# The feed-forward's weight loads moved to GpSimd's queue, and one string of TensorE's order replaced

## The chip, the cores and the metric

The kernel runs on one core of a Trainium2 chip. The metric is device time in microseconds (us), the median of several runs. A core has five engines with instruction streams of their own: TensorE (PE; its weight loads are shown as PEld), VectorE (DVE), ScalarE (ACT), GpSimd (POOL) and SyncE (SP). They wait for one another by semaphores. Transfers between the chip's main memory and the core are issued by an instruction on one of these engines; in this kernel mostly by SyncE, a few by ScalarE and GpSimd. An engine works through its own instructions strictly in order, so a transfer whose wait is not over holds what stands behind it on that engine.

## The reference

Two rounds of a recurrent attention layer and a gated feed-forward layer, with the same weights in both rounds:

```
x = x + A(layernorm(x));  x = x + B(layernorm(x))
x = x + A(layernorm(x));  x = x + B(layernorm(x))        x: 1 x 2048 x 576, bf16

A: 64 segments of 32 tokens, one after the other; mem is 8 x 576
   h = concat(mem, segment)                 40 tokens
   q, k, v = h Wq, h Wk, h Wv               32 heads of 128
   p = softmax(mask(q k^T / sqrt(128)));  o = (p v) Wo
   mem = o[:8];  output = o[8:]

B: out = (silu(x w1) * (x w3)) w2           576 -> 4608 -> 576
```

The memory of 8 tokens makes the 64 segments of one attention layer a chain. The two rounds can overlap: the second round can work on a segment once the first round has finished it.

## The kernel before

**Steps.** Both rounds run interleaved. At step t the first round works on segment t and the second on segment t - 8, so there are 72 steps; in 56 of them both rounds are present. A step goes through the 32 heads in four groups of eight. For each group TensorE makes q and k (`QK`), the scores (`SC`), the product of the softmax with v (`PV`) and the output projection (`WO`). Between `SC` and `PV` the softmax runs: VectorE adds the mask and subtracts the maximum, ScalarE takes the exponential, VectorE sums and writes the normalised result into the tile PB, and PB is transposed into the tile PTS. In steps with both rounds that transpose is a DMA transpose issued by SyncE (`ptr_dma`, line 1223). After it has landed, GpSimd clears PB again (`pb_zero`, line 1213). PB and PTS have two buffers each.

**Feed-forward.** Every four steps a job (`job`) puts 128 tokens of each round through the feed-forward. The 4608 hidden columns are cut into 18 pairs of 256 columns. For each pair three nodes load weights: `W13` (two transfers of 512 rows of 256 columns, from w1 and w3), `W13t` (two transfers of the last 64 rows) and `W2l` (one transfer of 256 rows of 576 columns). So a job has 90 weight transfers. The tiles `w13`, `w13t` and `w2` have two buffers each, so the load of a pair waits until TensorE is through with the pair two before it. In the trace the tiles of w1 and w3 stand as W<-in_B_w_dram, that of w2 as W2C<-in_B_w_dram. The last job is different: its weights go into the room of the attention weights (`tail_load`).

**Order.** A planner (`plan`) fixes the order of all instructions before the program is built. Every piece of work is a node with an engine, a duration, a latency `lat` after its end and a priority. TensorE's order is not planned but written out as a string, one letter for each node: Q and q for the q and k products, S for scores, P for `PV`, O and o for `WO`, F and f for a pair's products with w1 and w3, W and w for the products with w2, G, g, V and v for the products that make v, n, a and b for the transposes after a layer norm, p for the attention output's transposes. The whole string is FIRST, then eleven times FOUR, then LAST. FOUR is one period: four steps and one job, 208 letters. The other engines' nodes are put, one after the other, where they can start soonest by the planner's durations; among those that can start, the one with the lowest priority number goes first. `TRLAT` is the latency that the planner gives a DMA transpose after its 1.25 us on the queue. The chip keeps the order of every engine; the times are then its own.

**Queues.** SyncE issues the weights at the start, the feed-forward's weights, the DMA transposes and most loads of x. GpSimd computes the power in the layer norms (`ln_pow`, line 889), clears PB, loads the residual XR and stores finished output (line 719). TensorE's instructions stand under line 704, ScalarE's under 707, VectorE's under 710, SyncE's transfers under 713: these lines are helpers that every operation goes through, so the tiles tell operations apart.

Of the kernel before, what the change touches and what calls it, by code (L numbers as in the profile page):

```python
# [13 lines left out]
P = 128  # L14
R64 = 64
D = 576
# [16 lines left out]
R_HT = 6  # L33
PTR = 112
PRE = ()
TRLAT = 3.0
AHEAD = True
BACK = 4
GATES = {1: "WO1", **{i: "WO3" for i in range(2, 8)}}
# [177 lines left out]
def ewh(*ns):  # L217
# [11 lines left out]
    "SQQqqqQSbQGSgqqQPQGSgOPGggOPGwOoPooOo"  # L229
)  # L230
FOUR = (
    "QQppQqqqqQvVSnSnQFfqqQQFqqffFQWSwPSFffPFOOWowoPFffPOOwoFoWQQQqqqfFSFqqfqQQQwSWGSFqfqgQQPGSfggwGPFPOGWogOPOOoooFV"
    "vfqqQQWQQqqfSFSqqQQwQSFffqqFQPwOSWPFFPoffOOwPWOoooFqqfqQQWQQSaqqQSbqqqQQQSwSGggGPGPOoggGPOPOOooo"
)
LAST = (
    "QqqqppQQQqSvVSnnQQqqfFSqqQPQFSffOPFOwPWFOfFoPoofOoWQQQqqqwSQFQqqfGSqgQQPQqfSFGgqgPGSWwfFOFPOfgGOwoPOoooqqqQQQQqS"
# [9 lines left out]
class Opt:  # L246

    qk, qkt, sc, tr, pv, wo, wog, vm = 0.0079, -0.0342, 0.0268, 0.1447, 0.0406, 0.2653, 0.0725, 0.1407
    vmt, vx, vxt, ff, fft, win, w2, gstep = -0.0231, 0.2313, 0.0843, 0.2124, -0.1839, 0.8 * (LAG - 4), 0.1943, 0.0624
# [3 lines left out]
def make_nodes(em, nseg, pools, o=Opt, dma_bw=230e3, load_bw=380e3, tail_bw=330e3):  # L253
# [4 lines left out]
    def node(*a, **k):  # L258
        n = Node(*a, **k)
        n.prio += 1e-9 * len(nodes)  # L260
        nodes.append(n)
        return n
# [27 lines left out]
    b = banks(1)  # L290
# [208 lines left out]
    def job(j):  # L499
# [24 lines left out]
        def units(pps, at0, end):  # L524
            for at, pp in enumerate(pps, at0):
                mids, w2s, htts, lds = [], [], [], []
                stays = last and pp == npp - 1
                in_tail = end and not stays
                for pr_ in (2 * pp, 2 * pp + 1):
                    prio = (s0 + 4 if end and not last else s0) + o.ff + (o.win if s0 + 4 < nst else o.last_win) * (2 * at + pr_ % 2) / NPR  # L530
                    if stays:
                        w13, w13t, w2 = kept[pr_]
                        ld = ldt = []
                        w2s.append(w2)
                    elif in_tail:
                        w13 = w13t = w2 = None
                        ld = ldt = tail[pp]
                    else:
                        keep = before_last and pp == npp - 1
                        w13, w13t, w2 = Slot("w13", users=1 + keep), Slot("w13t", users=1 + keep), Slot("w2", users=ne + keep)  # L540
                        kept[pr_] = w13, w13t, w2
                        after = stored if j == 0 else first_ld[:1]
                        ld = [node("DMA", 0.98, em.load_w13(pr_, w13), deps=after, prio=prio - 1, acq=[w13], lat=3.1, name="W13")]
                        ldt = [node("DMA", 1.03, em.load_w13t(pr_, w13t), deps=after, prio=prio - 0.995, acq=[w13t], lat=3.0, name="W13t")]
                        first_ld.extend(ld)
                        lds.append(node("DMA", 0.45, em.load_w2(pr_, w2), deps=after, prio=prio - 0.99, acq=[w2], lat=2.95, name="W2l"))
                        w2s.append(w2)
                    b = banks()
                    htt = Slot("htt", users=ne)
# [130 lines left out]
class Emitter:  # L680
# [34 lines left out]
    def adma(self, out, in_):  # L715
        self.ch("ACT", self.nc.scalar.dma_start(out=out, in_=in_))

    def swdma(self, out, in_):
        self.ch("POOL", self.nc.gpsimd.dma_start(out=out, in_=in_))

# [85 lines left out]
    def load_w13(self, pr, w13):  # L806
        def f(n):
            fa = pr * 2 * P
            W = self.T.W13[:, w13.i]
            for kind, wd in ((0, self.a.w1), (1, self.a.w3)):  # L810
                self.dma(W[:, 4 * kind:4 * kind + 4], wd[0:4 * P, fa:fa + 2 * P].rearrange("(c p) f -> p c f", p=P))
        return f

    def load_w13t(self, pr, w13):
        def f(n):
            fa = pr * 2 * P
            for kind, wd in ((0, self.a.w1), (1, self.a.w3)):
                self.dma(self.T.W13[kind * R64:(kind + 1) * R64, w13.i, 8], wd[4 * P:D, fa:fa + 2 * P])
        return f

    def load_w2(self, pr, w2):
        fa = pr * 2 * P
        return lambda n: self.dma(self.T.W2C[:, w2.i], self.a.w2[fa:fa + 2 * P, :].rearrange("(b p) d -> p b d", p=P))

    def tail_load(self, i, what, gate):

# [739 lines left out]
```

## Time and profile before

| | |
|---|---|
| median of 3 runs | 2702.18 us (2692.01 to 2706.06) |
| profiled execution | 2702.11 us, its span 2700.2 us |
| mean granted TensorE clock | 0.987 |
| TensorE busy | 2582.1 us, 96% |
| VectorE busy | 2039.5 us, 76% |
| ScalarE busy | 1202.9 us, 45% |
| GpSimd busy | 334.3 us, 12% |
| transfers | 371.40 MB, 138 GB/s |

All rows below come from one profiled execution. A row of a timeline gives the start in us from the span's beginning, the length in us, the engine (a q behind it means that its sequencer issues a transfer), the line, the operation, the tiles as written<-read, the shape, and how many instructions were merged; a square bracket tells how long the engine stood idle before it and what ended that. A row of waits gives the engine that waited, what it waited for, the us in total, how often, and the longest. A row of a tile gives an engine, its operation and tiles, how many, and the least, median and greatest length in ns. A row of transfers gives tiles, the issuing engine, how many, KB each, and the median us from issue to landing. A row of stretches gives start and end, the length, the busy time of PE, PEld, DVE, ACT and POOL (with their instructions), the granted TensorE clock in parts of one, the share of the DMA engines that was busy, and GB/s. The chain that ended last is followed back from the last instruction; its shares are of the whole span.

### The profile page before, as it was taken

Reading aid. Unit: us, or ns where it says so; the run is one execution under the profiler, and the core shown is the slowest. Engines: PE = TensorE matmul, PEld = TensorE weight load, DVE = VectorE, ACT = ScalarE, POOL = GpSimd, SP = SyncE. Lnnn points to the kernel's source line nnn. Section 1 sums busy time; section 2 is a strip of 40 time slices with the busy share of each in tenths; the row PEclk is TensorE's granted clock in tenths of the full one; section 3 lists DMA queues with packets and bytes.
Section 4 is the critical chain, followed back from the end, with each engine's and each line's share of the span. In section 5 each row is a group of like instructions: output and inputs, shape, how many; then the busy total and the mean of one; then the engine's idle time right before and its main releaser. Section 6 shows DMA issues by size and latency. Waiting matters only on the chain.

```text
span 2700.2 us, 132038 instructions
## 1 busy us (share of the span) xinstructions
PE 2582.1 (96%) x58710; PEld 2202.3 (82%) x58766; DVE 2039.5 (76%) x5185; ACT 1202.9 (45%) x3447; POOL 334.3 (12%) x399
## 2 busy tenths in 40 slices
PE   6999999999999999999999999999999999999998
PEld 4787878888788888888888888887888888888876
DVE  4777777777777777787777877777777787787876
ACT  2554443434444343454535444453444445344443
POOL 1111011101101111110111101011110101011110
PEclk8999999999999999999999999999999999999999
DMA  9056745666544654555475655546555654554458
GB/s 312 8 163 157 170 88 139 137 144 137 115 128 103 163 131 127 149 114 129 111 165 125 148 129 124 135 106 153 124 146 130 130 134 102 128 146 124 130 149 247
DMA packets 690428, 371.40 MB, mean 138 GB/s; under 512 B 234328, under 2 KB 682592, under 8 KB 689216
## 3 DMA queue, kind: packets, MB, share of 16 engines
q1 hardware_dynamic: 686320, 355.08, 53.4%
q8 instruction: 459, 7.52, 1.2%
q0 software_dynamic: 3024, 6.93, 0.9%
q10 hardware_dynamic: 512, 0.94, 0.2%
q14 instruction: 113, 0.93, 0.1%
HBM read 306.72 MB, written 2.36 MB: 114 GB/s over the span
## 4 chain that ended last, share of the span: by engine, by line
PE 74%; DMA 9%; DVE 9%; issue 2%; SPq 1%; ACT 1%; POOL 0%; DVEq 0%; POOLq 0%; ACTq 0%
PE bank L704 74%; DMA PTS<-PB 7%; DVE HTT L710 2%; DVE PB L710 1%; DVE STAT L710 1%; DMA XN<-in_A_x_dram 1%; DVE SME L710 1%; DVE V L710 1%; SPq L713 1%; DVE XR L710 1%; DVE LNS L710 0%; DMA W<-in_B_w_dram 0%; DVE OT L710 0%; DVE QKT L710 0%; DMA W2C<-in_B_w_dram 0%
## 5 line engine op out<-in xcount | busy, mean ns | idle before, releaser
L704 PEld LDWEIGHTS <-W 128*128 128x128 bf16 (+2 forms) x32272 | 1253.0, 100 | 127.8 <-issue 67.9
L704 PE MATMUL bank<-HT,W 128*128 128x80 bf16 (+3 forms) x23040 | 784.8, 197 | 19.6 <-ACT HT L707 7.3
L704 PE MATMUL bank<-XTB,W 128*64 128x256 bf16 (+5 forms) x9232 | 667.6, 264 | 4.6 <-DMA W<-in_B_w_dram 2.7
L1213 POOL MEMSET PB<- 128x1024 bf16 x288 | 273.1, 952 | 1846.0 <-DMA PTS<-PB 1033.3
L707 ACT ACTIVATE QKT<-bank 128x192 bf16<-128x192 f32 (+2 forms) x1473 | 348.2, 323 | 303.8 <-PE bank L704 301.4
L704 PE MATMUL bank<-OT,WO 128*128 128x80 bf16 (+3 forms) x11520 | 418.7, 199 | 4.1 <-ACT OT L707 2.8
L704 PEld LDWEIGHTS <-WO 128*128 128x128 bf16 (+1 forms) x11520 | 389.0, 103 | 31.3 <-issue 20.8
L707 ACT ACTIVATE V<-bank 64x512 bf16<-64x512 f32 (+1 forms) x575 | 326.8, 586 | 188.7 <-PE bank L704 180.8
L704 PE MATMUL bank<-WV,HT 128*32 128x512 bf16 (+5 forms) x3442 | 363.5, 385 | 10.2 <-DMA WV<-in_A_Wv_dram 4.6
L707 ACT ACTIVATE HTT<-bank 128x512 bf16<-128x512 f32 (+1 forms) x324 | 176.3, 549 | 338.4 <-PE bank L704 333.3
L704 PE MATMUL bank<-W2C,HTT 128*64 128x288 bf16 (+1 forms) x2992 | 323.6, 287 | 1.7 <-DVE HTT L710 0.4
L707 ACT ACTIVATE OT<-bank 128x320 bf16<-128x320 f32 (+2 forms) x406 | 156.5, 399 | 296.8 <-PE bank L704 292.5
L710 DVE TENSOR_TENSOR PB<-SME,STAT 40x128 bf16<-40x128 f32 (+4 forms) x912 | 274.9, 336 | 15.5 <-POOL PB L1213 5.9
L710 DVE TENSOR_REDUCE STAT<-SME 104x8 f32<-104x320 f32 (+1 forms) x576 | 273.3, 474 | 14.9 <-ACT SME L707 7.7
L710 DVE SCALAR_TENSOR_TENSOR XR<-bank,XR 128x288 f32<-128x288 f32 x574 | 245.6, 448 | 50.4 <-PE bank L704 46.3
L704 PEld LDWEIGHTS <-HT 128*32 128x32 bf16 (+4 forms) x3496 | 151.5, 98 | 147.2 <-issue 39.9
L704 PEld LDWEIGHTS <-HTT 128*64 128x64 bf16 (+1 forms) x3072 | 225.6, 104 | 47.2 <-issue 7.6
L710 DVE SCALAR_TENSOR_TENSOR HTT<-HTT,bank 128x512 bf16<-128x512 bf16 (+1 forms) x324 | 201.4, 622 | 72.6 <-ACT HTT L707 69.3
L710 DVE CAST V<-bank 64x512 bf16<-64x512 f32 (+1 forms) x289 | 197.8, 685 | 61.2 <-PE bank L704 55.6
L710 DVE TENSOR_TENSOR HTT<-HTT,bank 128x512 bf16<-128x512 bf16 (+1 forms) x324 | 203.4, 628 | 28.1 <-PE bank L704 0.5
L707 ACT ACTIVATE SME<-SME 104x320 f32<-104x320 f32 (+1 forms) x288 | 135.2, 469 | 144.3 <-DVE SME L710 140.8
L710 DVE CAST QKT<-bank 128x128 bf16<-128x128 f32 (+4 forms) x447 | 124.8, 327 | 82.0 <-PE bank L704 80.9
(59 smaller groups left out, 1409.6 us busy)
## 6 DMA issues: line engine op xcount, KB each, us to landing
W<-in_B_w_dram SPq DMA_DIRECT2D x608, 256.0 KB, 3.7
W2C<-in_B_w_dram SPq DMA_DIRECT2D x304, 288.0 KB, 3.5
W<-in_B_w_dram SPq DMA_DIRECT2D x608, 32.0 KB, 3.2
W<-in_B_w_dram SPq DMA_DIRECT2D x16, 512.0 KB, 8.5
WO<-in_A_Wo_dram SPq DMA_DIRECT2D x4, 1152.0 KB, 10.3
XR<-in_A_x_dram POOLq DMA_DIRECT2D x16, 288.0 KB, 3.2
WV<-in_B_w_dram SPq DMA_DIRECT2D x8, 576.0 KB, 7.2
W<-in_A_Wq_dram SPq DMA_DIRECT2D x16, 256.0 KB, 6.7
```

Of the source, the lines that this page charges most:

```text
L704: self.ch("PE", self.nc.tensor.matmul(out, lhsT=lhsT, rhs=rhs, start=start, stop=stop, skip_group_check=True, **k))
L707: self.ch("ACT", self.nc.scalar.activation(*a, **k))
L710: self.ch("DVE", getattr(self.nc.vector, fn_)(*a, **k))
L713: self.ch("SP", self.nc.sync.dma_start(out=out, in_=in_))
L1213: return lambda n: self.ch("POOL", self.nc.gpsimd.memset(self.T.PB[:, pb.i, 0:GROUPS[g][1]], 0.0))
```

## The change

Three constants, the string FOUR, and one new function. The 90 weight transfers of a job, and those of all jobs but the last one's own loads, are issued by GpSimd (`swdma`) and no longer by SyncE (`dma`). Their nodes stand in the planner under POOL with durations 1.2, 1.2 and 0.6 us (`LT`) for `W13`, `W13t` and `W2l`. `TRLAT` goes from 3.0 to 2.2. FOUR is another string of the same letters in the same numbers; FIRST and LAST stay. The buffers, the computation and the last job's loads stay. Every other engine's order follows from the planner, so it moves too.

```
-TRLAT = 3.0
+TRLAT = 2.2
+LOADS = "POOL"
+LT = (1.2, 1.2, 0.6)
...
 FOUR = (
-    "QQppQqqqqQvVSnSnQFfqqQQFqqffFQWSwPSFffPFOOWowoPFffPOOwoFoWQQQqqqfFSFqqfqQQQwSWGSFqfqgQQPGSfggwGPFPOGWogOPOOoooFV"
-    "vfqqQQWQQqqfSFSqqQQwQSFffqqFQPwOSWPFFPoffOOwPWOoooFqqfqQQWQQSaqqQSbqqqQQQSwSGggGPGPOoggGPOPOOooo"
+    "QQppQqqqqQVvSnnSQFqqffFQQQSqqWwPFPOOffoFSFoPwWffFOFPwOWooFqffQQQQqqqWSwSqqQQQQfqgqGSFPFfgGOSPFogfgGGPOOPWwOoooFv"
+    "VfqqQQQwWQfqqSFSQQQfqqqFSFqfPQwOSWoPFffOFPwOPWOoooFfqqqQQWQQSaqqQSbqqqQQQSGSgggGPGPOwGogPOPOOooo"
 )
...
-                        ld = [node("DMA", 0.98, em.load_w13(pr_, w13), deps=after, prio=prio - 1, acq=[w13], lat=3.1, name="W13")]
-                        ldt = [node("DMA", 1.03, em.load_w13t(pr_, w13t), deps=after, prio=prio - 0.995, acq=[w13t], lat=3.0, name="W13t")]
+                        ld = [node(LOADS, LT[0], em.load_w13(pr_, w13), deps=after, prio=prio - 1, acq=[w13], lat=3.1, name="W13")]
+                        ldt = [node(LOADS, LT[1], em.load_w13t(pr_, w13t), deps=after, prio=prio - 0.995, acq=[w13t], lat=3.0, name="W13t")]
...
-                        lds.append(node("DMA", 0.45, em.load_w2(pr_, w2), deps=after, prio=prio - 0.99, acq=[w2], lat=2.95, name="W2l"))
+                        lds.append(node(LOADS, LT[2], em.load_w2(pr_, w2), deps=after, prio=prio - 0.99, acq=[w2], lat=2.95, name="W2l"))
...
+    def wdma(self, out, in_):
+        (self.swdma if LOADS == "POOL" else self.dma)(out, in_)
...
-                self.dma(W[:, 4 * kind:4 * kind + 4], wd[0:4 * P, fa:fa + 2 * P].rearrange("(c p) f -> p c f", p=P))
+                self.wdma(W[:, 4 * kind:4 * kind + 4], wd[0:4 * P, fa:fa + 2 * P].rearrange("(c p) f -> p c f", p=P))
```

`load_w13t` and `load_w2` change from `self.dma` to `self.wdma` in the same way.

More of the change, by code (lines that the diff above doesn't have):

```diff
@@ L817, in f @@
             for kind, wd in ((0, self.a.w1), (1, self.a.w3)):
-                self.dma(self.T.W13[kind * R64:(kind + 1) * R64, w13.i, 8], wd[4 * P:D, fa:fa + 2 * P])
+                self.wdma(self.T.W13[kind * R64:(kind + 1) * R64, w13.i, 8], wd[4 * P:D, fa:fa + 2 * P])
         return f
@@ L822, in load_w2 @@
         fa = pr * 2 * P
-        return lambda n: self.dma(self.T.W2C[:, w2.i], self.a.w2[fa:fa + 2 * P, :].rearrange("(b p) d -> p b d", p=P))
+        return lambda n: self.wdma(self.T.W2C[:, w2.i], self.a.w2[fa:fa + 2 * P, :].rearrange("(b p) d -> p b d", p=P))
     def tail_load(self, i, what, gate):
```

## The prediction

> **What bounds the kernel now.** I read the page first (busy times, then the chain that ended last), then the stretches of the steady part, then TensorE's waits there.
>
> ```profile
> PE 2582.1 (96%) x58710; PEld 2202.3 (82%) x58766; DVE 2039.5 (76%) x5185; ACT 1202.9 (45%) x3447; POOL 334.3 (12%) x399
> PE bank L704 74%; DMA PTS<-PB 7%; DVE HTT L710 2%; DVE PB L710 1%; DVE STAT L710 1%; DMA XN<-in_A_x_dram 1%; DVE SME L710 1%; DVE V L710 1%; SPq L713 1%; DVE XR L710 1%; DVE LNS L710 0%; DMA W<-in_B_w_dram 0%; DVE OT L710 0%; DVE QKT L710 0%; DMA W2C<-in_B_w_dram 0%
> ```
> ```profile
> core 0: us, PE busy (x) PEld busy (x) DVE busy (x) ACT busy (x) POOL busy (x), PEclk, DMA share, GB/s
> 618.50:2188.80 1570.30, 1530.26 (x33020) 1311.45 (x33060) 1201.09 (x3031) 703.98 (x2120) 187.45 (x220) 0.99 0.56 132
> 778.70:939.70 161.00, 155.22 (x3302) 132.57 (x3306) 120.29 (x304) 70.40 (x212) 18.68 (x23) 0.98 0.55 129
> 1251.30:1405.60 154.30, 151.92 (x3303) 130.53 (x3307) 120.10 (x304) 70.27 (x212) 18.55 (x22) 1.00 0.58 133
> ```
> ```profile
> PE bank L704 <- DMA PTS<-PB: 28.7, 17, 3.8
> PE bank L704 <- ACT HT L707: 3.4, 10, 0.3
> ```
>
> TensorE bounds it: 96% busy, 74% of the chain. The largest transfer in the chain is the transpose of the softmax result (PTS<-PB, 7%). The first stretch is ten of the eleven repeats of the period: 157.0 us each, 153.0 busy, 4.0 idle. The last fence is TensorE's waits in that stretch: 28.7 of the 40.0 idle us are waits for that transpose, the next wait is 3.4. The other two stretches are a slow and a quick period. The slow one is busy 155.2 us against 151.9 for the same instructions, at a granted clock of 0.98 against 1.00; so what idles TensorE also seems to cost clock. All ten lie (1530.3 - 1519.2) / 10 = 1.1 us above the quick one in busy time.
>
> Why the transpose is late shows in SyncE's queue, with VectorE and TensorE beside it, in one period:
>
> ```profile
> 1656.74 1.22 SPq L1223 DMA_TRANSPOSE PTS<-PB  x1
> 1658.08 5.09 SPq L713 DMA_DIRECT2D W<-in_B_w_dram  x8
> 1663.28 1.26 SPq L1223 DMA_TRANSPOSE PTS<-PB  x1
> ```
> ```profile
> 1657.46 1.13 DVE L710 TENSOR_TENSOR PB<-SME,STAT 40x128 bf16<-40x128 f32 x4
> ```
> ```profile
> 1655.31 1.91 PE L704 MATMUL bank<-XTB,W 128*128 128x256 bf16 x16
> 1657.15 0.46 PE L704 MATMUL bank<-HT,W 64*128 64x80 bf16 x16
> 1660.88 1.15 PE L704 MATMUL bank<-W2C,HTT 128*128 128x288 bf16 x8
> 1668.60 0.71 PE L704 MATMUL bank<-PTS,V 128*128 128x80 bf16 x8 [2.39 <-DMA PTS<-PB]
> ```
>
> PB is written by 1658.59, but SyncE is issuing eight weight loads (5.09 us) and comes to the transpose at 1663.28, 4.7 us late. TensorE then stands for 2.39 us. In the period before it is the same place, with 1.77 us:
>
> ```profile
> 1502.13 4.77 SPq L713 DMA_DIRECT2D W<-in_B_w_dram  x8
> 1512.04 0.46 PE L704 MATMUL bank<-PTS,V 128*128 128x80 bf16 x8 [1.77 <-DMA PTS<-PB]
> ```
>
> **The change, part by part.** The sum is made against the profiled execution: 2702.1 us with a span of 2700.2; the median of the runs is 2702.2, so no correction.
>
> *1. SyncE's queue loses 1520 loads.* The stall above goes: I take 2.0 us a period, between 1.77 and 2.39. It is 20 of the 28.7 us in ten periods. What is late next is the rest, 0.9 us a period, from transposes that were issued in time and landed late. Of the 1.1 us of busy time lost with the clock I give back the same share, 0.8. Gain 2.8 us a period; bounds 0 (something else ends the wait at the same moment) and 2.9 + 1.1 = 4.0.
>
> *2. The order.* The letters of the period are the same 208, so TensorE's work is the same. Counting array shapes along the two orders, 63 changes of shape become 61. One costs about 0.1 us: sixteen matmuls of 256 columns, at an estimated 0.11 us, fill 1.73 of the 1.84 us between 1655.31 and 1657.15. So 0.2 us. The new order was made with a latency after a transpose of 2.2 us instead of 3.0, so products with V stand about 1 us nearer behind their scores. That eats slack and is priced under 3.
>
> *3. GpSimd gets the loads.* Their price there is not in the trace; the nearest rows are its own transfers, and SyncE's of several shapes:
>
> ```profile
> L719 POOL DMA_DIRECT2D out_dram<-XN x15: 549/552/594, 538.8 to 2667.3; - x15
> L713 SPq DMA_DIRECT2D out_dram<-XN x2: 366/372/377, 2697.1 to 2697.6; - x2
> L713 SPq DMA_DIRECT2D W<-in_B_w_dram x1248: 367/514/2909, 48.1 to 2685.1; - x179
> L713 SPq DMA_DIRECT2D W2C<-in_B_w_dram x304: 367/421/1792, 54.5 to 2648.9; - x152
> L1213 POOL MEMSET PB<- x288: 946/952/961, 32.3 to 2652.4; 128x1024 bf16 x144
> XR<-in_A_x_dram POOLq DMA_DIRECT2D x16, 288.0 KB, 3.2
> PTS<-PB SPq DMA_TRANSPOSE x224, 3.9
> ```
>
> GpSimd's own have 128 runs and take 0.55 us. The w1 and w3 loads have 512 runs, their tails 64, w2 256. If a load costs the same whatever its runs, it is 0.55 us; if all of it goes with the runs, 2.2, 0.28 and 1.1. On SyncE the least of both groups of weight loads (367 ns) is that of the 128-run store (366), so I take a value near flat: 0.6 to 0.8 us. A period has 18 x 5 = 90 loads: 54 to 72 us, on top of GpSimd's 18.7, in 154. At the other end it is 36 x 2.2 + 36 x 0.28 + 18 x 1.1 = 109 us. Neither fills the engine, so the price lies in who stands behind the loads.
>
> The Trainium skill, "DMA: Bandwidth & Descriptors", section "Anatomy of one DMA", says that many descriptors can be emitted before their incremental cost shows; its "SBUF — State Buffer", section "SBUF: two separate sides", warns that VectorE in a two-port mode keeps GpSimd from writing descriptors. By the first the sum stands at the forecast below; by the second it goes to rival B. The trace agrees with the first so far: beside a VectorE that is busy 76%, GpSimd's stores stay within 549 to 594 ns and its memsets within 946 to 961.
>
> Behind the loads stand the memsets that clear PB (16 a period), the power of the layer norms, the loads of XR and the stores. PB has two buffers, so in a burst of four groups the next softmax waits for the memset:
>
> ```profile
> 1591.40 1.85 POOL L1213 MEMSET PB<- 128x1024 bf16 x2 [29.81 <-DVE STAT L710]
> 1592.38 0.11 DVE PB L710
> ```
>
> The chain that ended last runs from the first memset (1591.40 + 0.96) straight into VectorE's next write of PB. In GpSimd's order in the changed program, memsets stand right behind four to twelve loads, 2 to 7 us of issue at 0.6. The same kind of hold on SyncE (4.7 us) reached TensorE with 2.39, half. A memset is one step further away, so I take 0.8 us a period for memset delays and for the nearer products together; bounds 0 and 2.4 (one such place in each period as bad as the old one).
>
> Steady part: -2.8 - 0.2 + 0.8 = -2.2 us a period, x 11 = -24.
>
> *4. The parts whose order is not searched anew.* From 149 to 618 us TensorE waits 12.5 us for transposes, after 2188.8 it waits 1.8:
>
> ```profile
> PE bank L704 <- DMA PTS<-PB: 12.5, 10, 3.9
> PE bank L704 <- DMA PTS<-PB: 1.8, 2, 1.3
> ```
>
> With the 70% of part 1, 9 to 10 us could go; the loads fall where that order did not foresee them on GpSimd, so I take 4. Bounds -12 and +8 (0.8 us more in ten such stretches).
>
> *5. The start.* Nothing holds the first ten loads on GpSimd any more, whereas SyncE had them behind all attention weights:
>
> ```profile
> 39.94 8.10 SPq L713 DMA_DIRECT2D WO<-in_A_Wo_dram  x4
> 48.08 6.40 SPq L713 DMA_DIRECT2D W<-in_B_w_dram  x4
> 5.47 0.30 POOL L1519 MEMSET maskb<- 8x40 bf16 x2
> 11.52 0.56 POOL L889 TENSOR_TENSOR LNS<-LNS,mhalf 128x1 f32<-128x1 f32 x1 [5.75 <-DVE LNS L710]
> 36.74 1.04 PE L704 MATMUL bank<-WV,HT 128*32 128x512 bf16 x8 [1.84 <-DMA WV<-in_A_Wv_dram]
> W<-in_B_w_dram SPq DMA_DIRECT2D x608, 256.0 KB, 3.7
> GB/s 312 8 163 157 170 88 139 137 144 137 115 128 103 163 131 127 149 114 129 111 165 125 148 129 124 135 106 153 124 146 130 130 134 102 128 146 124 130 149 247
> ```
>
> They now start at 5.8 us and compete with the weights that TensorE is waiting for (WV at 36.74). Two pairs are 2 x (512 + 64 + 288) KB = 1.77 MB; at 312 GB/s, the page's rate of the first slice, 5.7 us. Ten at 0.55 end at 11.3, just ahead of the layer norm's power at 11.52; at 2.2, 2.2, 0.28, 0.28, 1.1 they end at 17.9 and hold it 6.4 us. I take +5, bounds 0 and +12.
>
> Sum: -24 - 4 + 5 = -23: 2702 - 23 = 2679 us, 0.9% less.
>
> **The rivals.**
>
> *A: nothing gained, because the transposes land as late as before.* Other transfers in flight may slow a transpose whoever issued them. This speaks for it: a transpose at 1473.45 with only GpSimd's two transfers issued beside it frees its memset at 1478.94, 5.5 us later, against the median of 3.9.
>
> ```profile
> 1473.45 4.37 SPq L1223 DMA_TRANSPOSE PTS<-PB  x2
> 1473.68 0.57 POOL L719 DMA_DIRECT2D XR<-in_A_x_dram  x1
> 1474.25 0.55 POOL L719 DMA_DIRECT2D out_dram<-XN  x1
> 1478.94 1.84 POOL L1213 MEMSET PB<- 128x1024 bf16 x2 [4.14 <-DMA PTS<-PB]
> ```
>
> The order that counts on quicker ones then turns its missing microsecond into stalls at two or three places a period: about 2 us, which takes the gain of part 1 back. 2702 - 11 x (2.8 + 0.2 - 0.8 - 2.0) - 4 + 5 = 2701. Against it: the largest stall is plainly one of issue. The Trainium skill, "DMA: Bandwidth & Descriptors", section "Issuing engines are not separate DMA queues", states this rival as a rule: another issuing engine saves only the sequencer's time. The 4.7 us above are just that time, so by the rule the hold goes and the late landings stay. Chance 0.2.
>
> *B: slower, because GpSimd issues too slowly.* The tightest reuse of a w13 buffer in the new order has, between the end of one pair's product and the start of the next but one, a full product (1.84), two blocks of the W2 kind (1.0 each) and some 1.1 of small work: 4.9 us. In it two loads must be issued and the second must land: 2c + (3.2 - 0.57) + 0.14. That fits up to c = 1.07 us a load. At c = 1.5, with a memset (0.95) ahead, it is short by 1.8 us; with six places nearly as tight at some 1.2, 7 us a period: 2679 + 77 = 2756. At 2.2 it is 2.3 us short before any memset, towards 2820. For it: four times the runs; against it: the flat SyncE rows. Chance 0.25.
>
> *C: everything goes.* All 4.0 us of stalls and clock of part 1, no hold of memsets: 2702 - 11 x 4.2 - 10 + 5 = 2651. Chance 0.15.
>
> **How the numbers follow.** My forecast has 0.4. It takes C with it on the faster side: 0.55. About 0.5% (13.5 us) is what a measurement of this kernel can tell from no change. A lies inside it, 0.2; B beyond, 0.25. The range runs from 2648, C with the start at 2, to 2742, B at about c = 1.3; that leaves out the worse half of B and little of C. The forecast's own range is 2662 to 2690.
>
> **What would show it.** Right: the transpose's wait of 28.7 us falls to some 10 in the same ten periods; none of SyncE's transposes follows a load; GpSimd's busy time grows from 334 to about 1,250 to 1,450 us; the period is 154 to 155.5 us; the first product with WV comes some 5 us later. Wrong in B's way: GpSimd over 2,000 us busy, w1 and w3 loads over 1.1 us each, TensorE waiting for W<-in_B_w_dram. Wrong in A's way: transposes still land after 3.9 us in the median and the wait on them stays near 28.

## The result and the profile after

The changed kernel takes 2768.7 us (median of 4 runs, 2756.19 to 2776.68), the kernel before 2697.1 us beside it (4 runs): 1.0255 times as long, with a 95% interval of 1.0211 to 1.0299. Measured again later, the ratio was 1.0325 (1.0291 to 1.0359). The forecast was 2679 us and the range ended at 2742. The profiled execution took 2770.15 us with a span of 2768.3 us, 68.1 us more than the span before.

The first fence is the page after: TensorE's and GpSimd's busy time and the two large queues, then the chain that ended last. Lines of the code have moved a little: TensorE stands under 706, SyncE's transfers under 715, the DMA transposes under 1228, the clearing of PB under 1218, GpSimd's transfers under 724.

```profile
PE 2591.4 (94%) x58622; PEld 2213.0 (80%) x58678; DVE 2039.2 (74%) x5206; ACT 1210.6 (44%) x3426; POOL 1329.4 (48%) x1919
q0 software_dynamic: 95440, 275.99, 34.8%
q1 hardware_dynamic: 233968, 86.02, 17.9%
PE bank L706 59%; DMA PTS<-PB 12%; DMA W<-in_B_w_dram 4%; DVE PB L712 3%; DVE STAT L712 3%; DVE HTT L712 2%; DVE SME L712 1%; DVE V L712 1%; DMA W2C<-in_B_w_dram 1%; DVE XR L712 1%; POOL W L724 1%; ACT V L709 1%; DVE OT L712 1%; ACT OT L709 0%; POOL PB L1218 0%
```

The loads did move: GpSimd's queue (q0) now carries 276 MB and GpSimd is busy 1329 us. The clock is 0.986 (0.987 before), and TensorE's busy time has grown by only 9 us. The transpose's share of the chain has grown from 7% to 12%, and W<-in_B_w_dram, 0% before, has 4%. The next two fences have TensorE's waits: over the whole span before, then over the whole span after and, in the last two rows, after in the stretch from 618 to 2189 us, which the prediction looked at.

```profile
PE bank L704 <- DMA PTS<-PB: 43.1, 29, 3.9
...
PE bank L704 <- DMA W<-in_B_w_dram: 2.7, 5, 0.8
...
PE bank L704 <- DVE XN L710: 2.5, 2, 1.9
```
```profile
PE bank L706 <- DMA PTS<-PB: 74.8, 50, 3.6
PE bank L706 <- DMA W<-in_B_w_dram: 19.3, 29, 1.7
PE bank L706 <- DVE XN L712: 8.3, 4, 6.2
...
PE bank L706 <- DMA PTS<-PB: 54.1, 35, 3.6
PE bank L706 <- DMA W<-in_B_w_dram: 11.3, 16, 1.6
```

Over the whole span TensorE waits 74.8 us for transposes (43.1 before), 19.3 for the weights of w1 and w3 (2.7 before) and 8.3 for XN, the layer norm's output (2.5 before). That is 54 us more; the 9 us of busy time make it 63 of the 68. In the stretch where the wait for transposes was to fall from 28.7 to some 10 us, it nearly doubled.

The transposes themselves place the loss in time. The fence has them of before and then of after: count, least, median and greatest issue, first and last start, and their landing.

```profile
L1223 SPq DMA_TRANSPOSE PTS<-PB x224: 1221/1237/2222, 246.6 to 2415.9; - x112
DMA to landing us min/median/max: 2.9/3.9/6.7
```
```profile
L1228 SPq DMA_TRANSPOSE PTS<-PB x224: 1221/1224/2667, 258.5 to 2477.4; - x112
DMA to landing us min/median/max: 2.9/4.1/8.1
```

Up to the first transpose the changed kernel loses 11.9 us, from the first to the last 49.6 (2218.9 for 2169.3), after it 6.6. So the period is what counts: from the 33rd transpose to the 209th, eleven periods, it is 161.4 us (566.6 to 2341.8) instead of 156.9 (557.3 to 2282.7). The median landing has hardly grown, but the slowest takes 8.1 us for 6.7.

One late transpose of the changed kernel shows how it comes: SyncE, GpSimd and TensorE at 1390 us.

```profile
1390.34 1.24 SPq L1228 DMA_TRANSPOSE PTS<-PB  x1
```
```profile
1389.09 1.42 POOL L724 DMA_DIRECT2D W2C<-in_B_w_dram  x2 [1.09 <-PE bank L706]
1390.51 1.07 POOL L724 DMA_DIRECT2D W<-in_B_w_dram  x2
1392.49 2.60 POOL L724 DMA_DIRECT2D W<-in_B_w_dram  x4 [0.91 <-issue]
1397.51 0.95 POOL L1218 MEMSET PB<- 128x1024 bf16 x1 [2.42 <-DMA PTS<-PB]
```
```profile
1397.42 0.45 PE L706 MATMUL bank<-PTS,V 128*128 128x80 bf16 x8 [3.10 <-DMA PTS<-PB]
```

The transpose is issued as soon as PB is written; nothing holds it. But two loads of w2 went out 1.25 and 0.5 us before it and two tails of w1 and w3 0.17 and 0.7 us after it, and it lands 7.0 us later (PB's clearing and TensorE both go on at 1397.4). In the kernel before, SyncE issues these loads and the transpose one after the other, and none during the 1.25 us of the transpose's issue.

### The profile page after: what moved, and what is told of

The parts are those of the page before. It is cut to its first block, busy times and chain, and to the rows that moved or that the text cites. A ratio compares the mean times of both kernels' runs of the same rounds, so it can differ in the third digit from the quotient of the medians.

```text
span 2768.3 us, 132052 instructions
## 1 busy us (share of the span) xinstructions
PE 2591.4 (94%) x58622; PEld 2213.0 (80%) x58678; DVE 2039.2 (74%) x5206; ACT 1210.6 (44%) x3426; POOL 1329.4 (48%) x1919
## 3 DMA queue, kind: packets, MB, share of 16 engines
q0 software_dynamic: 95440, 275.99, 34.8%
## 4 chain that ended last, share of the span: by engine, by line
PE 59%; DMA 16%; DVE 11%; issue 4%; ACT 2%; POOL 1%; SPq 0%; DVEq 0%; POOLq 0%; ACTq 0%
PE bank L706 59%; DMA PTS<-PB 12%; DMA W<-in_B_w_dram 4%; DVE PB L712 3%; DVE STAT L712 3%; DVE HTT L712 2%; DVE SME L712 1%; DVE V L712 1%; DMA W2C<-in_B_w_dram 1%; DVE XR L712 1%; POOL W L724 1%; ACT V L709 1%; DVE OT L712 1%; ACT OT L709 0%; POOL PB L1218 0%
## 5 line engine op out<-in xcount | busy, mean ns | idle before, releaser
L724 POOL DMA_DIRECT2D W<-in_B_w_dram x1216 | 784.3, 650 | 407.3 <-PE bank L706 371.4
L706 PE MATMUL bank<-XTB,W 128*64 128x256 bf16 (+5 forms) x9232 | 670.3, 263 | 21.5 <-DMA W<-in_B_w_dram 19.3
L709 ACT ACTIVATE QKT<-bank 128x256 bf16<-128x256 f32 (+4 forms) x1429 | 336.9, 328 | 326.1 <-PE bank L706 320.4
L706 PE MATMUL bank<-OT,WO 128*128 128x80 bf16 (+3 forms) x11520 | 426.4, 200 | 3.4 <-ACT OT L709 2.8
L706 PEld LDWEIGHTS <-WO 128*128 128x128 bf16 (+1 forms) x11520 | 399.1, 103 | 32.4 <-issue 19.0
L709 ACT ACTIVATE V<-bank 32x512 bf16<-32x512 f32 (+1 forms) x597 | 336.6, 585 | 141.6 <-PE bank L706 136.0
L724 POOL DMA_DIRECT2D W2C<-in_B_w_dram x304 | 219.1, 723 | 238.4 <-PE bank L706 235.6
L706 PE MATMUL bank<-W2C,HTT 128*128 128x288 bf16 (+1 forms) x2904 | 318.2, 289 | 2.2 <-DMA W2C<-in_B_w_dram 1.7
L706 PEld LDWEIGHTS <-HTT 128*128 128x128 bf16 (+1 forms) x2984 | 224.9, 104 | 45.8 <-DVE HTT L712 4.7
L712 DVE CAST V<-bank 32x512 bf16<-32x512 f32 (+1 forms) x267 | 182.8, 685 | 64.8 <-PE bank L706 59.4
```

The source lines that it names most:

```text
L706: self.ch("PE", self.nc.tensor.matmul(out, lhsT=lhsT, rhs=rhs, start=start, stop=stop, skip_group_check=True, **k))
L709: self.ch("ACT", self.nc.scalar.activation(*a, **k))
L712: self.ch("DVE", getattr(self.nc.vector, fn_)(*a, **k))
```

## The experiments

Working figures that come from many rows of a trace are mine: for each of some 150 transposes in the ten periods from the fourth on, the hold (from the last write of the transpose's own PB tile to its issue), the landing (from issue to landed), and how many feed-forward loads start between 0.6 us before and 1.0 us after its issue ("near loads"). They are means; another choice of the stretch moves them by up to 0.2 us. The ratio is the time against the kernel before on the same chip, with its 95% interval. The two waits are TensorE's for transposes and for the weights of w1, w3 and w2, over the whole span.

| kernel | loads on, string | near loads | hold + landing, us | waits, us | ratio |
|---|---|---|---|---|---|
| before | SyncE, old | 0.1 | 0.73 + 3.87 = 4.60 | 43.1, 3.0 | 1 |
| order only | SyncE, new | 0.1 | 0.56 + 3.83 = 4.39 | 49.6, 11.0 | 1.0001 (0.998-1.0021) |
| loads only | GpSimd, old | 1.1 | 0.15 + 5.19 = 5.34 | 64.1, 30.7 | 1.0171 (1.0131-1.0211) |
| after | GpSimd, new | 1.1 | 0.15 + 4.41 = 4.56 | 74.8, 21.0 | 1.0255 (1.0211-1.0299) |
| short pause | GpSimd, old | 1.0 | 0.15 + 5.08 = 5.23 | 54.8, 19.6 | 1.0136 (1.01-1.0172) |
| short pause | GpSimd, new | 0.9 | 0.15 + 4.36 = 4.51 | 64.7, 34.5 | 1.0253 (1.0217-1.0289) |
| long pause | GpSimd, old | 0.7 | 0.15 + 4.79 = 4.94 | 61.2, 28.2 | 1.0209 (1.017-1.0248) |
| long pause | GpSimd, new | 0.9 | 0.15 + 4.27 = 4.42 | 65.4, 47.4 | 1.0293 (1.0243-1.0342) |
| one order | GpSimd, old | 0.3 | 1.25 + 3.77 = 5.02 | 60.7, 21.9 | 1.0182 (1.0165-1.0199) |
| one order | GpSimd, new | 0.4 | 1.12 + 3.69 = 4.81 | 72.6, 16.6 | 1.0181 (1.0166-1.0196) |
| halved loads | SyncE, old | 0.2 | 1.94 + 3.57 = 5.51 | 94.5, 24.2 | 1.0418 (1.0378-1.0459) |

**The parts apart.** The first kernel has the loads on GpSimd with the old string, the second the new string with the loads on SyncE.

```
 (from after)                      (from before)
-TRLAT = 2.2                      -TRLAT = 3.0
+TRLAT = 3.0                      +TRLAT = 2.2
-FOUR = (the new string)          -FOUR = (the old string)
+FOUR = (the old string)          +FOUR = (the new string)
```

> The loads on GpSimd as in the changed kernel, but the old string and the old latency of 3.0. Theory R (transposes land later because the loads now travel in another queue beside them, in packets of 4096 bytes instead of 512): the median landing stays near the changed kernel's 4.1 us, a tenth of them over 6 us, the kernel is still slower than before, about 2725 to 2745 us. Rival O (the new string is what hurts: it stands 1 us too close behind the scores): with the old string the loss goes, 2680 to 2705 us. Both: the start costs the same 10 to 12 us as in the changed kernel.

> The new string and the latency of 2.2, the loads back on SyncE. Theory R: landings are those of before (median 3.9 us), the holds on SyncE are back, TensorE's wait for transposes is somewhat over before's 43 us, time 2700 to 2730 us. Rival O: the string alone brings most of the loss, 2745 us or more.

The loads alone: 2751.2 us, 1.0171. The order alone: 2706.6 us, 1.0001. So the move of the loads costs by itself, and the string by itself nothing; with the loads on GpSimd it takes the ratio from 1.017 to 1.026 or more. The landing of the loads-only kernel:

```profile
DMA to landing us min/median/max: 2.9/5.0/11.0
```

So there is an exchange: the hold on SyncE's queue goes (0.73 to 0.15 us), and the landing grows by more (3.87 to 5.19). The softmax itself is not later: from the end of the scores to PB's last write it takes 6.3 us before, 6.4 with the loads alone and 6.2 in the changed kernel.

For the changed kernel the mean says nothing: hold and landing are 4.56 us together, 4.60 before. But TensorE waits at only a few of the sixteen transposes of a period. Counted from the 49th transpose, with ten periods added up, 22.9 of the 27.4 us of waits before lie at the second place; its transpose is held for 4.9 us, and it is the stall that the prediction showed. In the changed kernel this place has 1.0 us. Instead the fourth has 20.4 us (the transpose at 1390 us is one of these; 11.5 with the new string alone) and the sixteenth 22.9, of 55.6. The sixteenth shows the cause best. With the new string and the loads on SyncE it has no near load, lands after 2.9 us, and TensorE never waits for it. In the changed kernel it has 1.8 near loads and lands after 5.5 us. With the long pause described below and the new string, it has none again, lands after 3.1 us, and the wait is 1.2 us.

**The start.** In the plan the loads of the first job now wait for the last load of the output projection's weights (`ld_o`), behind which SyncE's queue had them; the changed kernel was also run once more.

```
-                        after = stored if j == 0 else first_ld[:1]
+                        after = ld_o[-1:] if j == 0 else first_ld[:1]
```

> The changed kernel, with the first ten weight loads planned behind the attention weights, so that on GpSimd they stand behind the first layer norm's power and four memsets. If the start is a separate loss of 10 to 12 us (6 us of bandwidth, 4 to 5 us of the held power), the time is 2756 to 2760 us and the first product with WV stands within 1 us of before's 32.5 us; if the loss at the start is absorbed later, the time stays near 2769.

> The changed kernel once more, beside its own variants on one chip. The late start of the weights gave 2790 us where 10 us less than 2769 was expected, though on every engine the order after the start is the same. If that was the chip, this run is near 2790 too; if a shift of the start truly costs, it stays at 2755 to 2775, some 2.1 to 3.0% over before.

2789.7 us (1.0315; 1.0279 to 1.0351) against 1.0255 and, in the repeat, 1.0325 for the changed kernel. The first product with WV comes at 32.8 us instead of 38.2 and the first transpose at 249 instead of 258, and at the end no gain can be seen. Whether the cost of the early loads is absorbed later was not shown. The two ratios of the changed kernel differ by nearly twice an interval's half width, so ratios that were not measured side by side are compared only roughly here. Loads only, order only and this kernel ran on one chip: 1.0171, 1.0001 and 1.0315.

**What slows a transpose.** Three probes leave the whole computation out: 16 transposes of each setting on SyncE, alone or with four 256 KB loads from one queue.

```
+    for eng, wide in ((None, 0), ("SP", 0), ("ACT", 0), ("ACT", 1), ("POOL", 0), ("POOL", 1)):
...
+    for eng, lead in ((None, 0), ("SP", -1), ("ACT", -1), ("POOL", -1), ("POOL", 0), ("POOL", 1), ("ACT", 1)):
...
+    for n, at in ((4, "before"), (4, 0), (4, 512), (4, 1024), (4, 1536), (1, "before"), (2, "before")):
```

> Leaves out the whole computation (zeros are stored) and measures the disputed cost by itself: 16 transposes of the kernel's shape in each of six settings: alone; behind four 256 KB loads on SyncE's own queue; beside the same four loads from ScalarE's queue; beside two 512 KB loads with rows of 4096 bytes from ScalarE's queue; beside the four loads from GpSimd; beside the two wide loads from GpSimd. Theory R in its form 'size of packets': alone 2.9 us; SyncE 5 to 6; ScalarE with 512-byte rows 4 to 5; the other three, all with 4096-byte packets, 6 to 8. Form 'software queue': only GpSimd's two are at 6 to 8, ScalarE's two alike at 4 to 5. Form 'any other queue': ScalarE's two and GpSimd's two alike, all over SyncE's. Rival O: GpSimd's are no later than SyncE's.

> Leaves out the computation, as the first probe. 16 transposes in each of seven settings: alone; with four 256 KB loads issued behind the transpose on SyncE's own queue; with the four loads issued by ScalarE, and by GpSimd, about 1.3 us after the transpose; by GpSimd at the same time (lead 0.5 us); by GpSimd, and by ScalarE, about 2 us before it. Theory Q (on one queue what stands behind a transpose can't delay it, on another queue it can): alone 2.9, SyncE behind under 3.4 us; ScalarE and GpSimd behind 4 to 5.5; at the same time 5.9 as before; ahead 5 to 6. Rival (only what is already in flight matters): all three loads-behind settings alike, under 3.5 us.

> Leaves the whole computation out: only transposes of PB with loads beside them, 16 of each setting. Four 256 KB loads from GpSimd ahead of the transpose, then four that start about 0.4, 0.6, 0.8 and 1.0 us after it, then one and two loads ahead. Theory W: landing falls from 5-6 us (ahead) in steps to 2.9 as the loads start later, and is 2.9 from about 1.1 us on; one load ahead costs about 0.7 us, two 1.4. Rival (in flight at any time counts): landing stays over 4 us in all settings with four loads.

Medians in the first: alone 2.90 us; behind four loads on SyncE's own queue 5.38 (after a hold of 1.28); beside four from ScalarE 6.26, from GpSimd 5.86; beside two loads with rows of 4096 bytes 5.37 (ScalarE) and 5.95 (GpSimd). So neither the software queue as such nor the size of the rows is the cause. In the second, loads that start 1.1 us or more after the transpose leave it at 2.90 to 2.97 on all three queues; ahead of it they cost 2 to 3 us on ScalarE's and GpSimd's. The third finds the edge. The fence has the transposes and their landing, for four loads of GpSimd of which the first starts 0.28 us before, then 0.31, 0.58 and 0.85 us after the transpose; the others follow 0.74 us apart.

```profile
L60 SPq DMA_TRANSPOSE PTS<-PB x16: 1222/1223/1329, 6.5 to 133.4; - x16
DMA to landing us min/median/max: 5.4/5.8/6.2
...
L60 SPq DMA_TRANSPOSE PTS<-PB x16: 1222/1222/1224, 141.6 to 265.0; - x16
DMA to landing us min/median/max: 4.9/5.1/5.5
...
L60 SPq DMA_TRANSPOSE PTS<-PB x16: 1222/1222/1224, 273.3 to 399.4; - x16
DMA to landing us min/median/max: 4.6/4.9/5.3
...
L60 SPq DMA_TRANSPOSE PTS<-PB x16: 1222/1222/1354, 407.7 to 533.9; - x16
DMA to landing us min/median/max: 2.9/2.9/3.6
```

Loads of which the first starts up to 0.58 us after the transpose still cost it 2 us; if it starts at 0.85, they cost nothing. One load just ahead costs 1.1 us (4.0), two 2.2 (5.1 to 5.2). A transpose takes SyncE 1.22 us to issue, so a load behind it on its own queue can't start inside that window.

**Clearing PB, and the planner's durations.** Two kernels drop the clearing of PB in steps with both rounds (the expectations took the output to become wrong; the stale values turned out not to be used), from after and from before. A third gives the planner of before longer durations for the loads.

```
-        return lambda n: self.ch("POOL", self.nc.gpsimd.memset(self.T.PB[:, pb.i, 0:GROUPS[g][1]], 0.0))
+        return lambda n: None if self.both(t) else self.ch("POOL", self.nc.gpsimd.memset(self.T.PB[:, pb.i, 0:GROUPS[g][1]], 0.0))
...
-    ld = [node("DMA", 0.98, ...)]; ldt = [node("DMA", 1.03, ...)]; lds.append(node("DMA", 0.45, ...))
+    ld = [node("DMA", 1.09, ...)]; ldt = [node("DMA", 1.18, ...)]; lds.append(node("DMA", 0.51, ...))
```

> The changed kernel without the memsets that clear PB in the 56 steps with both rounds: stale numbers of another step stay in the columns that a step doesn't write, so the output is wrong, the work of the other engines is the same. Theory M (on GpSimd the loads stand behind memsets that wait for a transpose, so weights come late): TensorE's wait for W falls from 19 to under 8 us, and the gain is at least 20 us more than the same cut brings in the kernel before. Theory Q (the loss is the slower landing beside loads of another queue): the transposes land as late as before the cut, and both kernels gain alike, 5 to 25 us each from the shorter way from a transpose to the next write of PB.

> The kernel before with the same cut (memsets of PB left out in the steps with both rounds, so the output is wrong in the same way): the yardstick for the run above. Both theories: 5 to 25 us faster than before, or the same.

> The kernel before, where the planner only is told longer issue times for the loads on SyncE, those of the trace (1.09, 1.18 and 0.51 us for a node instead of 0.98, 1.03 and 0.45), so that a transpose may come ahead of a load in SyncE's queue. If the hold of 4.7 us can be had away without another queue, TensorE's wait for transposes falls from 43 to under 30 us and the time to 2670 to 2695; if the order on SyncE stays what it is, nothing moves.

After without the clearing: 1.0348 (1.0324 to 1.0372), no better than 1.0325. Before without it: 0.9987 (0.997 to 1.0004). Longer durations: 0.9993 (0.9973 to 1.0012). Clearing PB behind the loads on GpSimd isn't the loss, and neither is the planner's view of the loads.

**Two queues the other way round.** The loads stay on SyncE, and ScalarE issues the transposes.

```
-                tr = node("DMA", 1.25 * nh / 8, em.ptr_dma(...), ..., name="TR", lat=TRLAT)
+                tr = node("ACT", 1.25 * nh / 8, em.ptr_dma(...), ..., name="TR", lat=TRLAT)
```

> The kernel before, with the DMA transposes issued by ScalarE instead of SyncE; the loads stay on SyncE, in their 512-byte packets. Theory G (a transpose that waits at the head of SyncE's queue keeps the loads back, so that little is in flight when it goes; on any other queue the loads run ahead of it): the holds vanish, and the mean landing rises from 3.9 us to 4.4 or more, as with GpSimd's loads, a tenth over 6 us; with 1.2 us of ScalarE for each, no faster than before: 2705 to 2760 us. Rival S (it is the software queue, or what GpSimd's late issue does): landings stay at 3.9 or fall, and the kernel gains some 20 us from the holds, 2675 to 2695.

2738.9 us, 1.0126 (1.0094 to 1.0157): no GpSimd queue and no dearer load, and the transposes land after 4.88 us in the mean, with 1.1 near loads each. The landing goes with the separate queues, not with GpSimd. The time of this run is another matter: the waits for transposes (37.6 us) are below those of before. ScalarE also pays 224 issues, and TensorE's waits for ScalarE grow from 13.6 to 20.5 us, for VectorE from 16.9 to 28.1, for the weights from 3.0 to 15.0.

**A pause on GpSimd.** Before each transpose's place in its order GpSimd makes one-column multiplies, the first of which waits for PB's last write: two (0.34 us in the median) and then nine (1.35 us), each with the old and the new string.

```
+            for i in range(2):          # then range(9)
+                self.ch("POOL", self.nc.gpsimd.tensor_tensor(self.T.PACE[:, i:i + 1], self.T.mhalf[:], self.T.mhalf[:], op=ALU.mult))
+                if not i:
+                    self.tc.add_manual_dep(self.last["POOL"].ins, self.pbw[t, g].ins.name, self.pace_dep, reason="pace of the loads")
             self.ch(e, q.dma_start_transpose(...))
```

> Loads on GpSimd, old string, latency 3.0 (the run with the loads alone), and ahead of every DMA transpose, in GpSimd's planned order, a pair of one-column multiplies of about 0.55 us each, the first of which waits for the last write of PB: loads planned behind a transpose can't start before it, as on SyncE. Theory G: the mean landing falls from 5.15 us to 4.3 or less, and the time from 1.7% over before to within 0.8% of it. Rival S: landings as before the pacing, time the same or worse, since GpSimd only waits longer.

> The same pacing in the changed kernel (new string, latency 2.2). Theory G: mean landing from 4.4 us to 4.0 or less, and at least 20 us faster than the changed kernel on this chip. Rival S: no gain.

> Loads on GpSimd and the old string, as in the run with the loads alone, but nine one-column GpSimd multiplies before each transpose's place in GpSimd's order, the first of them waiting for PB's last write: 9 x 0.17 to 0.2 = 1.5 to 1.8 us in which GpSimd issues no load after the transpose has gone. The two multiplies of the earlier paced run took 0.34 to 0.51 us, and in its trace 1.0 load a transpose still started between 0.6 us before and 1.0 us after the transpose (before: 0.1). Theory W (SyncE's queue gave each transpose a window in which no load starts, and the loss comes from loads that start inside it): the loads in that window fall below 0.5, the mean landing from 5.0-5.3 us to 4.5 or less, TensorE's wait for the transposes from 55-64 us to 50 or less, and the time to 1.000-1.010 of before. Rival (loads issued from another queue slow the transposes whenever they are in flight, and come late themselves): landing 4.8 us or more, 1.012 or more.

> The changed kernel (new string, TRLAT 2.2) with the same nine multiplies before each transpose. Theory W: mean landing from 4.4 to 3.9 us, TensorE's wait for the transposes from 65-82 us to 50 or less, 1.000-1.015 of before. Rival: landing 4.3 or more, 1.02 or more. If the window works but the loads come too late behind it, the wait for W<-in_B_w_dram grows beyond 35 us.

None gets the loss back: 1.0136 and 1.0253 with the short pause, 1.0209 and 1.0293 with the long one. On average the near loads fell to 0.7 and 0.9 only, and landings by at most 0.4 us. The pause keeps back the loads behind the transpose; those ahead of it in the order often go at the same moment, since the transpose doesn't wait for GpSimd. With the long pause and the new string the sixteenth place is cured, but at the twelfth the landing is now 8.2 us, and TensorE waits 20.2 us there in ten periods (8.1 in the changed kernel). The long pause also makes the weights later (47.4 us of waits with the new string).

**One order on two queues.** Now the transpose also waits for the first multiply, so that it stands in GpSimd's order of loads as it stood in SyncE's.

```
+                    first = self.last["POOL"]
             self.ch(e, q.dma_start_transpose(...))
+            self.tc.add_manual_dep(self.last[e].ins, first.ins.name, self.pace_dep, reason="the transpose in the loads' order")
```

> As the run with nine multiplies and the old string, but eight of them, and the transpose on SyncE now also waits for the first one on GpSimd. So the loads that stand ahead of a transpose in the planned order go ahead of it, and those behind it start 1.2 us or more after it, as in one queue; only the queue that carries the loads differs from before. Theory W (what was lost is the one order of loads and transposes): loads from 0.6 us before to 1.0 us after a transpose fall from 0.7-1.0 to 0.3 or less, the mean landing from 4.9 to 4.2 us or less, PB's tile waits again before the transpose (0.7 to 1.5 us in the mean), TensorE's wait for the transposes falls from 61-64 to 50 us, and the time to 1.000-1.010. Rival (the software queue's loads are dearer or later in themselves, 0.65 to 0.75 us an issue instead of 0.5): the time stays at 1.014 or more even with landings of 4.2 us, with the hold over 1.5 us or the wait for W<-in_B_w_dram at 20 us or more.

> The changed kernel (new string, TRLAT 2.2) with the same one order of loads and transposes. Theory W: mean landing from 4.3-4.4 to 4.0 us or less, 1.000-1.012 of before. Rival: 1.02 or more.

1.0182 and 1.0181: theory W is right on the landing and wrong on the time. With the old string:

```profile
DMA to landing us min/median/max: 2.9/3.6/6.8
```
```profile
PE bank L706 <- DMA PTS<-PB: 60.7, 47, 3.3
PE bank L706 <- DMA W<-in_B_w_dram: 20.4, 25, 2.2
```

The median landing is 3.6 us, below the 3.9 of before. The near loads that are left all start more than 0.6 us after the transpose. But the hold is back, at 1.25 us instead of 0.73, and TensorE's two waits (60.7 and 21.9 us) are not far below those with the loads alone (64.1 and 30.7). This is the rival's case: 1.014 or more, with the wait for W<-in_B_w_dram at 20 us (20.4). The extra loss of the new string is gone: with one order both strings give the same. For the changed kernel that is a gain clear of the intervals (1.0181 instead of 1.0255 to 1.0325), for the loads alone none (1.0182, 1.0171).

**The price of an issue.** Last, the kernel before with SyncE's loads of w1, w3 and w2 cut in two, which makes them dearer on their queue and leaves them there.

```
-                self.dma(W[:, 4 * kind:4 * kind + 4], wd[0:4 * P, fa:fa + 2 * P]...)
+                for i in range(0, 4, 2):
+                    self.dma(W[:, 4 * kind + i:4 * kind + i + 2], wd[i * P:(i + 2) * P, fa:fa + 2 * P]...)
...
-        return lambda n: self.dma(self.T.W2C[:, w2.i], self.a.w2[fa:fa + 2 * P, :]...)
+            for b in range(2):
+                self.dma(self.T.W2C[:, w2.i, b], self.a.w2[fa + b * P:fa + (b + 1) * P, :])
```

> The kernel before, with SyncE's loads of w1, w3 and w2 each cut into two halves (256 rows of 256 columns, 128 rows of 576 columns), the same bytes in the same place of the order. SyncE's least issue is 0.37 us, so a load takes about 0.75 to 0.8 us of its queue instead of 0.51 and 0.42: the price that GpSimd's loads have (0.75 and 0.72). Theory I (what is left of the loss with one order, 1.018, is the dearer issue of each load, whoever issues it): the hold before a transpose grows from 0.73 to 1.1 us or more in the mean, TensorE's wait for W<-in_B_w_dram from 2.7 to 10 us or more, and the time to 1.008-1.02 of before. Rival (something else of the software queue): 0.998-1.005, and the rest of the loss stays open.

2822.4 us, 1.0418 (1.0378 to 1.0459):

```profile
PE bank L704 <- DMA PTS<-PB: 94.5, 56, 4.1
PE bank L704 <- DMA W<-in_B_w_dram: 17.6, 22, 1.8
```

Theory I holds in its direction, and the loss is twice its upper end: hold 1.94 us, weights waited for as on GpSimd. The landing (3.57 us) is no longer than before, so here the queue is the loss. TensorE's busy time grows too, by 50 us at a granted clock of 0.976 (0.987 before). Between 250 and 2300 us the issue of the feed-forward's loads takes 653 us of its queue before (943 x 0.564 + 236 x 0.514), 778 on GpSimd in the one-order kernel (934 x 0.651 + 234 x 0.725), and 937 here (1358 x 0.536 + 452 x 0.463). If the loss went with the added issue, the 4.18% for 284 us would make 1.84% for GpSimd's 125 us; 1.82% was measured. That is one proportion between runs on two chips, the one-order kernel also has its multiplies and a start that is 7 us later, and the cut doubles the number of transfers along with the price. So it is consistent and not proven.

## Why the prediction was wrong

*Step 1, "SyncE's queue loses 1520 loads", is the step that failed.* It read the stall rightly (a transpose that waits behind loads) and the hold did go, from 0.73 to 0.15 us. It then took the landing behind the hold for fixed and let the stall of 2.0 us a period vanish. In place of the hold came near loads: 1.1 a transpose instead of 0.1, and in the probe one load just ahead costs 1.1 us. With the loads alone it is 5.34 us from PB's write to the landing, 4.60 before. In the changed kernel the stall of the prediction went as forecast (22.9 to 1.0 us in ten periods), and two other places, whose transposes land late beside near loads, took 43 us. The term was a gain of 2.8 us a period, bounds 0 to 4.0; with the loads alone the period is 160.8 us and not 156.9 (the 33rd transpose at 571.8, the 209th at 2340.1), a loss of 3.9. The lower bound of 0 said that the worst was no gain; a loss was not excluded by any row, and the row of rival A (a transpose that took 5.5 us beside two of GpSimd's transfers, issued 0.2 and 0.8 us after it) pointed to this mechanism.

*The weights were left out of the sum.* TensorE's waits for W and W2C grow from 3.0 to 21.0 us in the changed kernel and 30.7 with the loads alone. The prediction had them in rival B alone, under another premise. A load costs GpSimd 0.65 us in the mean against 0.56 on SyncE, w2 0.72 against 0.51, and the 256 KB loads land after 4.2 us instead of 3.7.

*Step 2, "The order".* Right alone: 1.0001. That the nearer products eat slack was said, but the price was put under step 3 together with the memsets. With separate queues it is real (1.0315 against 1.0171 on one chip, with the later start; 1.0253 against 1.0136 and 1.0293 against 1.0209 with the pauses). Spread over eleven periods that is 2.1 to 3.5 us a period, where 0.8 was taken with an upper bound of 2.4. The reason is argued, not tested alone: products stand 11.8 us of TensorE's work behind their scores instead of 12.8, while the slowest transposes take 8.1 us.

*Step 3, "GpSimd gets the loads".* The issue price was right: 0.6 to 0.8 us near flat was taken, and it is this, for the loads of w1 and w3 and then of w2 (least, median, greatest ns):

```profile
L724 POOL DMA_DIRECT2D W<-in_B_w_dram x1216: 517/658/927, 5.7 to 2714.1; - x174
L724 POOL DMA_DIRECT2D W2C<-in_B_w_dram x304: 703/722/770, 8.4 to 2717.4; - x152
```

GpSimd is busy 1329 us; 1250 to 1450 were named. The part of the 0.8 us a period that was meant for late memsets is not there (no gain without them). So GpSimd was not too slow to fill the buffers, and rival B, whose time it came out at, was wrong in its premise of c over 1.07 us. Yet the 0.1 to 0.2 us more for each load may not be free either: the last two experiments agree with that and don't prove it. Of the hold by VectorE that the prediction named beside B nothing is seen: no load took over 0.93 us beside a VectorE that is busy 74%. Whether VectorE ever ran in the mode in question no run here shows.

*Step 4.* The waits for transposes from 149 to 618 us stayed at 12.5 us; 9 to 10 of them had been counted as what could go, and 4 taken. After 2189 us they are 8.2 instead of 1.8, though that stretch now also holds work of the last period.

*Step 5, "The start".* +5 us was right for the first product with WV (38.2 us for 32.5), but not for the reason in full:

```profile
13.78 0.54 POOL L724 DMA_DIRECT2D W<-in_B_w_dram  x1 [2.61 <-DMA W<-in_B_w_dram]
14.91 0.73 POOL L724 DMA_DIRECT2D W2C<-in_B_w_dram  x1 [0.59 <-DMA W<-in_B_w_dram]
15.71 0.57 POOL L894 TENSOR_TENSOR LNS<-LNS,mhalf 128x1 f32<-128x1 f32 x1
```
```profile
16.80 0.74 PE L706 MATMUL bank<-ident,XN 128*64 128x128 bf16 x10 [6.20 <-DVE XN L712]
```

The loads take eight semaphores in turn to tell of their landing, so the ninth load waits until the first has landed (at 13.5 us). The prediction had the ten go out unhindered. The layer norm's power behind them comes at 15.71 instead of 11.52; TensorE waits 6.2 us for XN. It was 11.9 us by the first transpose, and the late start, which got 9 of them back, was no faster at the end.

*The rivals.* A named what happened, other transfers in flight slow a transpose whoever issued them, but let it take back only the gain. The Trainium skill, "DMA: Bandwidth & Descriptors", section "Issuing engines are not separate DMA queues", has it that another issuing engine saves only the sequencer's time. The runs agree as far as it goes: the hold was all that could be saved. They add that the saved wait had also kept the loads back.

What stays open: how much of the changed kernel's 2.6 to 3.3% is landing, how much the loads' price and how much weights that come late. They can't be added up: the one-order kernels mend the landing and pay a longer hold. Whether the price of a load on GpSimd can be lowered was not tried. No kernel here beats the one before.

## What to carry to other kernels

A transfer that waits at the head of a busy queue is not only late: it also holds back what would slow it. Before such work is moved to a second queue, look at what starts in the microsecond around the transfer that matters, and count from "data written" to "landed" rather than the hold alone. Where a queue is on the path, its price for each issue counts too (on SyncE, 284 us more of issue went with 4.2% more time), so a dearer issue belongs into the sum even if the engine stays half idle. Ask also which of the transfers TensorE really waits for: a mean over all of them can stay the same while the two that matter get later.

## What the runs showed of the hardware

A DMA transpose of this shape takes 2.9 us alone. Loads that go ahead of it slow it, whichever of SyncE's, ScalarE's or GpSimd's queues they are on and whether their rows have 512 or 4096 bytes: 4.0 us with one 256 KB load just ahead, 5.1 with two, 5 to 6.3 with four. GpSimd's loads still do so (4.9) when the first starts 0.58 us after its issue, and no longer at 0.85 us (2.9). On SyncE's and ScalarE's queues loads that start 1.1 us or more after it don't slow it either.

GpSimd's queue moved the same bytes in far fewer packets: 95,440 on q0, while q1 fell from 686,320 to 233,968. Nothing here got quicker by it. Its issue takes 0.54 us for the 64-row tails, 0.72 for w2 (256 rows of 1152 bytes) and 0.76 for w1 and w3 (512 rows of 512 bytes), so eight times the rows of a tail cost 0.2 us.
